# Six whole-array f-tiles instead of four in the opening of a squared-ReLU MLP

## The chip, the cores and the metric

The kernel runs on one core of a Trainium2 chip. The metric is the device time of one execution in microseconds (us). The profile is one execution, with a span about 1.7 us shorter than that execution's time. PE is the matrix engine, PEld its weight loads, DVE the vector engine, ACT the scalar engine, SP the engine that issues most of the transfers.

## The reference, cut

```python
# x (1, 2048, 576), w1 (576, 4608), b1 (4608), w2 (4608, 576), b2 (576), all bf16
h = jnp.einsum("bsd,df->bsf", x, w1) + b1
r = jnp.where(h > 0, h, 0)
h = r * r
out = jnp.einsum("bsf,fd->bsd", h, w2) + b2
```

The first product contracts 576 = 4 x 128 + 64 rows. The hidden width 4608 is 36 "f-tiles" of 128. The 2048 rows of x are worked in four blocks of 512.

## The kernel before

In most of the first product an f-tile is contracted in nine slices of 64 rows, and two f-tiles run side by side in the two halves of the array ("row-tiled"):

```python
def a_part(b, j, bk, steps):                  # a pair of f-tiles, 18 matmuls of 64x512
    for i in steps:
        for h in range(2):
            c = ORDER[h][i]
            rows = slice(h * H, (h + 1) * H)
            nc.tensor.matmul(bk[h][:], lhsT=w1h[rows, c, j * P:(j + 1) * P], rhs=xT[b][rows, place(h, c), :],
                             start=(i == 0), stop=(i == NH - 1))
```

This needs x transposed and copied to both halves of the partitions, so the kernel cannot begin with it. Block 0 begins with G = 4 f-tiles in another form, here called the opening: x arrives in four row tiles (x0 to x3), PE transposes them chunk by chunk, and each transposed chunk of 128 rows meets whole-array weights (chunks 0 to 3, each 128 rows by G f-tiles). It works in two halves of 256 columns, so that it can begin when only x0 and x1 are there:

```python
load_x(nc.sync, 0);    load_x(nc.scalar, 1)      # x tiles and weight chunks alternate on two queues
load_quad(nc.sync, 0); load_quad(nc.scalar, 1)
load_quad(nc.sync, 2); load_x(nc.scalar, 2)
load_x(nc.sync, 3);    load_quad(nc.scalar, 3)
...                                              # cut: remainder rows, then the row-tiled weights by pairs
bk0 = [bank("ph") for _ in range(G)]             # G of the 8 PSUM banks

def full_mm(half, c):
    cols = slice(half * HALF, (half + 1) * HALF)
    for q in range(4):
        nc.tensor.matmul(bk0[q][:, cols], lhsT=qn[:, c, q * P:(q + 1) * P], rhs=xT[0][:, c, cols], ...)

transpose_chunks(0, (0,), (V,));  transpose_chunks(0, (1,), (A,))    # each needs a PSUM bank and a copy out
transpose_chunks(0, (2,), (A,));  transpose_chunks(0, (NC,), (V,))
full_mm(0, 0)
transpose_chunks(0, (3,), (A,))
full_mm(0, 1); full_mm(0, 2)
transpose_chunks(1, (0, 1), (V, A))              # needs x2 and x3
full_mm(0, 3)
transpose_chunks(1, (2, NC), (A, V))
full_mm(1, 0)
transpose_chunks(1, (3,), (V,))
full_mm(1, 1)
...                                              # cut: biases
full_mm(1, 2); full_mm(1, 3)
...                                              # cut: remainder rows (64), two f-tiles side by side
```

Five dummy products ("warm", NWARM = 5) keep PE busy from 0.4 to 2.7 us, while x0 is on its way. Results leave PSUM through ACT (ReLU with bias) and DVE (square). After all four blocks the second product follows.

Of the kernel before, what the change touches and what calls it, by code (L numbers as in the profile page):

```python
# [17 lines left out]
def kernel(  # L18
# [9 lines left out]
    nc = tc.nc  # L28
    P = 128
    H = 64  # L30
    x2 = x.flatten_outer_dims()
    out2 = out.flatten_outer_dims()
    S, D = x2.shape
    F = w1.shape[1]
    FH = F // 2
    G = 4
    NFT = F // P
    NJ = NFT // 2
    NC = D // P
    NH = D // H  # L40
    DM = NC * P
# [15 lines left out]
    def bank(name):  # L57
        return psum.tile([P, SB], FP32, name=name, tag="bank")
# [10 lines left out]
    def early(n):  # L69
        at[0] += n  # L70
        assert at[0] <= NFT * D
        return w2_sb[:, at[0] - n:at[0]]


    xT = [early(XW).rearrange("p (w s) -> p w s", s=SB) for b in range(NSB - 1)]
    xT3 = xpool.tile([P, NH, SB], BF16, name="xT3", tag="xT3")
    xT.append(xT3[:])
    xs = early(RT * D).rearrange("p (j c) -> p j c", c=D)
    qn = early(NC * 4 * P).rearrange("p (c f) -> p c f", c=NC)
    qr = early(2 * P)  # L80
    pairs = [(0, 2), (1, 3)] + [(f, f + G) for f in range(G, NFT) if (f // G) % 2]
    slot = {ft: (h, j) for j, pr in enumerate(pairs) for h, ft in enumerate(pr)}
    assert len(pairs) == NJ and len(slot) == NFT

# [9 lines left out]
    def load_quad(eng, c):  # L94
        eng.dma_start(out=qn[:, c, :], in_=w1[c * P:(c + 1) * P, 0:G * P])

    def load_w1(eng, h, j0, n, cs):
        f0 = pairs[j0][h] * P
        eng.dma_start(out=w1h[h * H:(h + 1) * H, cs, j0 * P:(j0 + n) * P], in_=w1_rows[:, cs, f0:f0 + n * P])
# [1 line left out]
    NWARM = 5  # L101

    def load_rest(eng, h):
        eng.dma_start(out=qr[h * H:(h + 1) * H, :], in_=w1[DM:D, 2 * h * P:2 * (h + 1) * P])

    b1T = const.tile([P, NFT], FP32, name="b1T")
    warm = const.tile([P, 1], FP32, name="warm")
# [9 lines left out]
    for h in range(2):  # L117
        load_rest(nc.sync, h)


    for j0, n in ((2, 1), (3, 1), (4, 1), (5, 1), (6, 1), (7, 1), (8, 2), (10, 2), (12, 2), (14, 4)):
        for h in range(2):
            load_w1(nc.sync, h, j0, n, slice(0, NH))

# [46 lines left out]
    def copy_psum(eng, dst, src):  # L171
        if eng is nc.scalar:
            nc.scalar.copy(out=dst, in_=src)
        else:
            nc.vector.tensor_copy(out=dst, in_=src)  # L175

    def transpose_chunks(half, cs, engs):
        tps = [psum.tile([P, HALF], BF16, name="tp", tag="bank") for c in cs]
        for i in range(2):
            for c, tp in zip(cs, tps):  # L180
                d0 = c * P if c < NC else D - P
                nc.tensor.transpose(tp[:, i * P:(i + 1) * P], xs[:, 2 * half + i, d0:d0 + P], ident[:])  # L182
        cols = slice(half * HALF, (half + 1) * HALF)
        for c, tp, eng in zip(cs, tps, engs):
            copy_psum(eng, xT[0][:, c if c < NC else 7, cols], tp[:])
            if c == NC:
                nc.vector.tensor_copy(out=xT[0][0:H, 8, cols], in_=tp[H:P, :])

    def hT_of(b, ft):
        if b < NSB - 1:  # L190
            return hT[b][:, ft, :].rearrange("p (j s) -> p j s", j=RT)
        h, j = slot[ft]
        return w1h[:, h * RT:(h + 1) * RT, j * P:(j + 1) * P]

    def evac_h(b, ft, bk):
        r = rpool.tile([P, SB], BF16, name="r", tag="r")
        nc.scalar.activation(out=r[:], in_=bk[:], func=ACT.Relu, bias=b1T[:, ft:ft + 1], scale=1.0)  # L197
        r3 = r[:].rearrange("p (j s) -> p j s", j=RT)
        nc.vector.tensor_tensor(out=hT_of(b, ft), in0=r3, in1=r3, op=ALU.mult)  # L199

    def place(hi, c):
        if hi:
            return c // 2 if c % 2 else (3 + c // 2 if c else 8)
        return 8 if c == 8 else (4 if c % 2 else 0) + c // 2
# [11 lines left out]
    def a_step(b, j):  # L216
        bk = [bank("ph") for _ in range(2)]
        a_part(b, j, bk, range(NH))
        for h in range(2):
            evac_h(b, pairs[j][h], bk[h])  # L220


    bk0 = [bank("ph") for _ in range(G)]

    def full_mm(half, c):
        cols = slice(half * HALF, (half + 1) * HALF)
        for q in range(4):
            nc.tensor.matmul(bk0[q][:, cols], lhsT=qn[:, c, q * P:(q + 1) * P], rhs=xT[0][:, c, cols],  # L228
                             start=(half == 0 and c == 0), stop=False, skip_group_check=True)

    V, A = nc.vector, nc.scalar
    transpose_chunks(0, (0,), (V,))
    transpose_chunks(0, (1,), (A,))
    transpose_chunks(0, (2,), (A,))
    transpose_chunks(0, (NC,), (V,))
    full_mm(0, 0)
    transpose_chunks(0, (3,), (A,))
    full_mm(0, 1)
    full_mm(0, 2)
    transpose_chunks(1, (0, 1), (V, A))  # L240
    full_mm(0, 3)
# [6 lines left out]
    nc.vector.tensor_copy(out=b1T[:], in_=b1T_ps[:, 0:NFT])  # L248
    full_mm(1, 2)
    full_mm(1, 3)  # L250
    for i in range(2):
        for h in range(2):
            rows = slice(h * H, (h + 1) * H)
            nc.tensor.matmul(bk0[2 * h + i][:], lhsT=qr[rows, i * P:(i + 1) * P], rhs=xT[0][rows, place(h, 8), :],  # L254
                             start=False, stop=True, skip_group_check=True)
    nc.vector.tensor_copy(out=xT[0][0:H, 4:7, :], in_=xT[0][H:P, 0:3, :])
    nc.vector.tensor_copy(out=xT[0][H:P, 4:7, :], in_=xT[0][0:H, 1:4, :])
    nc.vector.tensor_copy(out=xT[0][H:P, 8, :], in_=xT[0][0:H, 0, :])
    for q in range(G):
        evac_h(0, q, bk0[q])  # L260


    def load_xT(b):
# [3 lines left out]

    load_xT(1)
    for h in range(2):
        load_w1(nc.sync, h, 0, 2, slice(0, NH))  # L270
    for b in range(2, NSB):
        load_xT(b)
    w2_view = w2_dram.rearrange("(ft p) d -> p ft d", p=P)
# [2 lines left out]
    def load_w2(c, n=1):  # L276
        nc.sync.dma_start(out=w2_sb[:, c * W2CH * D:(c + n) * W2CH * D].rearrange("p (ft d) -> p ft d", d=D),
                          in_=w2_view[:, c * W2CH:(c + n) * W2CH, :])
# [9 lines left out]
    def finish_xT(b):  # L288
        nc.vector.tensor_copy(out=xT[b][0:H, 8, :], in_=xT[b][H:P, 7, :])
        nc.vector.tensor_copy(out=xT[b][H:P, 8, :], in_=xT[b][0:H, 0, :])  # L290

    for j in range(2, NJ):
        a_step(0, j)
        if j == NJ - 2:
            finish_xT(1)
    load_w2(0)
    for b in range(1, NSB):
        for j in (*range(2, NJ), 0, 1):
            a_step(b, j)
            if j == NJ // 2 and b + 1 < NSB:  # L300
                finish_xT(b + 1)
        if b == 1:
            load_w2(1)
        if b == 2:
            load_w2(2, 2)
# [63 lines left out]
```

## Time and profile before

| | before |
|---|---|
| median time, three runs | 290.14 us |
| span of the profile | 288.7 us |
| PE busy | 284.9 us (99%) |
| opening, from the second x tile to the first row-tiled product | 3.09 to 9.78 us of the chain |
| 1260 row-tiled products | 135.97 us |

The page of the kernel before, its first lines; the number after x counts instructions:

```profile
span 288.7 us, 4818 instructions
...
PE 284.9 (99%) x2067; PEld 133.7 (46%) x2078; DVE 79.5 (28%) x196; ACT 95.6 (33%) x153; POOL 1.5 (1%) x8
...
PE   9999999999999999999999999999999999999996
```

PE is busy in every slice, and no other engine comes near. A share does not say what PE waits for, so the next view matters more: the chain of waits of the kernel before (start, length, what; the share of "by line" left out):

```profile
0.21 2.84 DMA w_sb<-in_x_dram
3.04 0.05 issue
3.09 0.93 PE tp L182 x7
4.02 0.85 PE ph L228 x4
4.87 0.21 PE tp L182 x2
5.09 1.36 PE ph L228 x8
6.45 0.22 PE tp L182 x4
6.67 0.44 PE ph L228 x4
...
9.24 0.54 PE ph L254 x4
9.78 135.97 PE ph L213 x1260
145.75 15.66 PE pc L315 x144
```

L182 are transposes, L228 the 256-column products, L254 the remainder rows, L213 the row-tiled products. One wait for x1 ends at 3.04 us; after that each piece follows the last. Four products take 0.85 us early and 0.44 us late: PE's clock is halved at first. The trace's record of the granted clock begins with full clock at 5.95 us. (The page's clock row shows full speed from the start: it knows only that record. In the opening, read the clock from the spacing of equal instructions: 213 ns slow, 109 ns fast.)

### The profile page before, as it was taken

To read this page: it belongs to the slowest core of one execution; us is meant where nothing else is said; L and a number is where in the kernel's file an instruction comes from. 1 tells how busy PE (TensorE), PEld (TensorE's weight loads), DVE (VectorE), ACT (ScalarE), POOL (GpSimd) and SP (SyncE) were. 2 spreads that over 40 slices of the span, in tenths; PEclk is the share of its full clock that TensorE was granted. 3 is DMA by queue.
4 is the path that set the end of the run, shared out by engine and by line. 5 is a ranking of instruction groups with operands and counts; after the bars stand their busy time and mean duration, and the time that the engine had idled before them with its cause. 6 is when DMAs were issued, how large, how long until landed. Compare 5 with 4: busy or idle time off the path is not lost.

```text
span 288.7 us, 4818 instructions
## 1 busy us (share of the span) xinstructions
PE 284.9 (99%) x2067; PEld 133.7 (46%) x2078; DVE 79.5 (28%) x196; ACT 95.6 (33%) x153; POOL 1.5 (1%) x8
## 2 busy tenths in 40 slices
PE   9999999999999999999999999999999999999996
PEld 5544444444444444444445444444444444444454
DVE  1644454444445444444420011111100111111111
ACT  3666666766666676666620000000000000000000
POOL 2000000000000000000000000000000000000000
PEclk9999999999999999999999999999999999999999
DMA  7999999910400004300000100000000000000000
GB/s 200 205 190 204 172 185 208 321 50 2 122 3 0 3 2 142 106 0 2 0 2 19 20 20 20 20 23 5 15 20 23 20 20 20 23 20 22 20 23 20
DMA packets 35381, 18.01 MB, mean 62 GB/s; under 512 B 21652, under 2 KB 35360, under 8 KB 35360
## 3 DMA queue, kind: packets, MB, share of 16 engines
q1 hardware_dynamic: 34752, 17.14, 26.4%
q10 hardware_dynamic: 576, 0.56, 0.6%
q8 instruction: 16, 0.26, 0.4%
q14 instruction: 5, 0.04, 0.0%
q0 software_dynamic: 32, 0.01, 0.0%
HBM read 11.94 MB, written 2.36 MB: 50 GB/s over the span
## 4 chain that ended last, share of the span: by engine, by line
PE 98%; DMA 1%; issue 0%; DVE 0%; ACTq 0%
PE ph L213 47%; PE po L329 43%; PE pc L315 5%; PE ph L228 2%; DMA w_sb<-in_x_dram 1%; PE tp L182 1%; PE ph L254 0%; DVE o_sb L331 0%; PE b1T_ps L247 0%; ACTq L353 0%
## 5 line engine op out<-in xcount | busy, mean ns | idle before, releaser
L197 ACT ACTIVATE r<-ph,b1T 128x512 bf16<-128x512 f32 x144 | 91.0, 685 | 48.4 <-PE ph L213 46.4
L213 PE MATMUL ph<-w_sb,w1h 64*128 64x512 bf16 x936 | 101.2, 376 | 0.0
L213 PEld LDWEIGHTS <-w1h 64*128 64x128 bf16 x1260 | 61.3, 94 | 74.6
L329 PE MATMUL po<-w_sb,hT 128*128 128x512 bf16 x423 | 92.9, 379 | 0.5
L329 PEld LDWEIGHTS <-hT 128*128 128x128 bf16 x432 | 42.2, 98 | 51.2 <-issue 0.4
L199 DVE TENSOR_TENSOR hT<-r 128x512 bf16<-128x512 bf16 x108 | 46.0, 426 | 54.7 <-ACT r L197 54.2
L331 DVE TENSOR_TENSOR o_sb<-po,b_bc 128x512 bf16<-128x512 f32 (+2 forms) x17 | 11.2, 660 | 116.7 <-PE po L329 109.7
L213 PE MATMUL ph<-xT,w1h 64*128 64x512 bf16 x324 | 35.1, 376 | 0.0
L329 PE MATMUL po<-w_sb,w1h 128*128 128x512 bf16 (+2 forms) x178 | 31.2, 336 | 0.1
L329 PEld LDWEIGHTS <-w1h 128*128 128x128 bf16 x180 | 16.2, 98 | 15.3
L199 DVE TENSOR_TENSOR w1h<-r 128x512 bf16<-128x512 bf16 x36 | 15.3, 426 | 19.6 <-ACT r L197 19.5
L315 PE MATMUL pc<-hT,w_sb 128*64 128x512 bf16 x108 | 15.7, 379 | 0.0
L315 PEld LDWEIGHTS <-w_sb 128*64 128x64 bf16 x144 | 8.1, 110 | 7.6 <-issue 0.4
L315 PE MATMUL pc<-w1h,w_sb 128*64 128x512 bf16 x36 | 7.9, 379 | 0.0
L317 ACT ACTIVATE oc<-pc,b2T 128x512 bf16<-128x512 f32 x2 | 1.4, 687 | 13.7 <-PE pc L315 13.7
L325 DVE COPY o_sb<-oc 128x64 bf16<-128x64 bf16 x16 | 2.8, 172 | 9.3 <-DMA oc<-oc 9.3
L228 PE MATMUL ph<-w_sb 128*128 128x256 bf16 x32 | 5.3, 313 | 0.0
L228 PEld LDWEIGHTS <-w_sb 128*128 128x128 bf16 x32 | 3.4, 115 | 0.6
L175 DVE COPY w_sb<-tp 128x256 bf16<-128x256 bf16 x5 | 1.5, 292 | 5.9 <-PE tp L182 5.9
L182 PE MATMUL tp<-ident,w_sb 128*128 128x128 bf16 x20 | 2.7, 264 | 0.1
L169 PE MATMUL wps<-one 128*128 128x512 bf16 x5 | 2.3, 628 | 0.4 <-DVE one L144 0.4
L182 PEld LDWEIGHTS <-w_sb 128*128 128x128 bf16 x20 | 1.9, 118 | 1.4 <-DMA w_sb<-in_x_dram 1.2
(27 smaller groups left out, 10.7 us busy)
## 6 DMA issues: line engine op xcount, KB each, us to landing
w_sb<-in_w_dram SPq DMA_DIRECT2D x2, 1728.0 KB, 8.7
w1h<-in_w_dram SPq DMA_DIRECT2D x8, 288.0 KB, 5.9
out_dram<-o_sb SPq DMA_DIRECT2D x15, 144.0 KB, 1.8
w1h<-in_w_dram SPq DMA_DIRECT2D x12, 144.0 KB, 3.7
w_sb<-in_w_dram SPq DMA_DIRECT2D x2, 864.0 KB, 7.2
w1h<-in_w_dram SPq DMA_DIRECT2D x2, 576.0 KB, 11.2
w_sb<-in_x_dram SPq DMA_DIRECT2D x2, 144.0 KB, 3.4
w_sb<-in_x_dram ACTq DMA_DIRECT2D x2, 144.0 KB, 3.5
```

Source lines behind the costliest of these rows:

```text
L169: nc.tensor.matmul(wps[:], lhsT=ones[:, 0:P], rhs=ones[:], start=(i == 0), stop=(i == NWARM - 1))
L175: nc.vector.tensor_copy(out=dst, in_=src)
L182: nc.tensor.transpose(tp[:, i * P:(i + 1) * P], xs[:, 2 * half + i, d0:d0 + P], ident[:])
L197: nc.scalar.activation(out=r[:], in_=bk[:], func=ACT.Relu, bias=b1T[:, ft:ft + 1], scale=1.0)
L199: nc.vector.tensor_tensor(out=hT_of(b, ft), in0=r3, in1=r3, op=ALU.mult)
L213: nc.tensor.matmul(bk[h][:], lhsT=w1h[rows, c, j * P:(j + 1) * P], rhs=xT[b][rows, place(h, c), :], start=(i == 0), stop=(i == NH - 1))
L228: nc.tensor.matmul(bk0[q][:, cols], lhsT=qn[:, c, q * P:(q + 1) * P], rhs=xT[0][:, c, cols], start=(half == 0 and c == 0), stop=False, ski ...
L315: nc.tensor.matmul(pc[h * H:(h + 1) * H, :], lhsT=w2(ft, DM, D), rhs=hT_of(2 * pr + h, ft), start=(ft == 0), stop=(ft == NFT - 1))
L317: nc.scalar.activation(out=oc[:, pr, :], in_=pc[:], func=ACT.Identity, bias=b2T[:], scale=1.0)
L325: nc.vector.tensor_copy(out=o_sb[:, DM:D], in_=o_tr[pr][:, jj, h * H:(h + 1) * H])
L329: nc.tensor.matmul(po[:, 0:e - a], lhsT=hT_of(b, ft)[:, jj, :], rhs=w2(ft, a, e), start=(ft == 0), stop=(ft == NFT - 1))
L331: nc.vector.tensor_tensor(out=o_sb[:, a:e], in0=po[:, 0:e - a], in1=b2_bc[:, a:e], op=ALU.add)
```

## The change

Its intent: let six f-tiles start in the form that is ready first, so that there is more work between transposes and so that the row-tiled weights are needed later; the bytes ahead of them on the queue stay the same. The diff, cut to its core (tables of pairs, remainder loads and loop bounds follow G in the same way, and the six results leave PSUM in the order in which they are finished):

```diff
-    G = 4
+    G = 6
+    GP = G // 2
...
-    qn = early(NC * 4 * P).rearrange("p (c f) -> p c f", c=NC)
+    qn = early(NC * G * P).rearrange("p (c f) -> p c f", c=NC)
...
-    for j0, n in ((2, 1), (3, 1), (4, 1), (5, 1), (6, 1), (7, 1), (8, 2), (10, 2), (12, 2), (14, 4)):
+    for j0, n in ((3, 1), (4, 1), (5, 1), (6, 1), (7, 1), (8, 1), (9, 1), (10, 2), (12, 2), (14, 4)):
...
-    bk0 = [bank("ph") for _ in range(G)]
...
-        for q in range(4):
+        for q in range(G):
...
-    transpose_chunks(0, (1,), (A,))
+    transpose_chunks(0, (1,), (V,))
     transpose_chunks(0, (2,), (A,))
     transpose_chunks(0, (NC,), (V,))
+    bk0 = [bank("ph") for _ in range(G)]
...
-        load_w1(nc.sync, h, 0, 2, slice(0, NH))
+        load_w1(nc.sync, h, 0, GP, slice(0, NH))
...
-    for j in range(2, NJ):
+    for j in range(GP, NJ):
```

Six accumulators leave two PSUM banks for the transposes. They are allocated after the first four transposes, whose banks two of them take over.

More of the change, by code (lines that the diff above doesn't have):

```diff
@@ L78 @@
     xs = early(RT * D).rearrange("p (j c) -> p j c", c=D)
-    qn = early(NC * 4 * P).rearrange("p (c f) -> p c f", c=NC)
-    qr = early(2 * P)
-    pairs = [(0, 2), (1, 3)] + [(f, f + G) for f in range(G, NFT) if (f // G) % 2]
+    qn = early(NC * G * P).rearrange("p (c f) -> p c f", c=NC)
+    qr = early(GP * P)
+    pairs = [(i, GP + i) for i in range(GP)] + [(G + i, G + NJ - GP + i) for i in range(NJ - GP)]
     slot = {ft: (h, j) for j, pr in enumerate(pairs) for h, ft in enumerate(pr)}
@@ L103, in load_rest @@
     def load_rest(eng, h):
-        eng.dma_start(out=qr[h * H:(h + 1) * H, :], in_=w1[DM:D, 2 * h * P:2 * (h + 1) * P])
+        eng.dma_start(out=qr[h * H:(h + 1) * H, :], in_=w1[DM:D, GP * h * P:GP * (h + 1) * P])
     b1T = const.tile([P, NFT], FP32, name="b1T")
@@ L250 @@
     full_mm(1, 3)
-    for i in range(2):
+    for i in range(GP):
         for h in range(2):
             rows = slice(h * H, (h + 1) * H)
-            nc.tensor.matmul(bk0[2 * h + i][:], lhsT=qr[rows, i * P:(i + 1) * P], rhs=xT[0][rows, place(h, 8), :],
+            nc.tensor.matmul(bk0[GP * h + i][:], lhsT=qr[rows, i * P:(i + 1) * P], rhs=xT[0][rows, place(h, 8), :],
                              start=False, stop=True, skip_group_check=True)
@@ L258 @@
     nc.vector.tensor_copy(out=xT[0][H:P, 8, :], in_=xT[0][0:H, 0, :])
-    for q in range(G):
-        evac_h(0, q, bk0[q])
+    for i in range(GP):
+        for h in range(2):
+            evac_h(0, GP * h + i, bk0[GP * h + i])
     def load_xT(b):
@@ L297 @@
     for b in range(1, NSB):
-        for j in (*range(2, NJ), 0, 1):
+        for j in (*range(GP, NJ), *range(GP)):
             a_step(b, j)
```

## The prediction

> **What bounds the kernel now.** The matrix engine, without a hole. The chain of waits has one wait, the load of the second x tile (0.21 to 3.04 us); from 3.09 to 285.97 us it is all PE, but for "issue" bits of 0.05 us. The page has PE 99% busy. The opening (transposes, whole-array products of 256-column halves, remainder rows) takes 3.09 to 9.78 us in the chain; then 1260 row-tiled matmuls take 135.97 us, 107.9 ns each.
>
> **What the change moves.** One pair of f-tiles leaves the row-tiled steps of block 0 and joins the opening.
> - Removed: 18 row-tiled matmuls, 18 x 107.9 ns = 1.94 us.
> - Added: 16 whole-array matmuls of 256 columns (the chain has 0.44 us for 4, so 109 ns) and 2 remainder ones: 1.96 us.
> Net +0.02 us. Both forms fill the array, and the opening has no idle time that more products could fill, so I see no gain.
>
> **The clock.** The clock record grants full clock only from 5.95 us: four 256-column matmuls take 0.85 us before it, 0.44 us after. The Trainium skill ("TensorE: Matmul & The Clock Gate", Part 1) says that the window is free-running; I expect the step at about the same time, and a stall before it to cost half its length.
>
> **Transfers.** Each whole-array weight chunk grows from 128 to 192 KB. By the issues' landings, x0, x1, chunk 0 and chunk 1 landed at 2.66, 3.05, 3.45 and 3.76 us, chunk 2 at 4.88, x2 5.27, x3 5.73, chunk 3 5.90. From 3.76 to 5.90 us 544 KB landed: 253 KB per us. The skill ("DMA: Bandwidth & Descriptors", Queues, rings and completion order) says that each DMA engine takes turns between queues, so chunk 0 pays for part of chunk 1. Estimates at that rate: chunk 0 at 3.8 us, chunk 1 4.3, chunk 2 5.6, x3 6.7, chunk 3 6.9. First uses, from the durations: chunk 0 at 3.71 us (slack before: 0.26 us), chunk 1 about 5.1, chunk 2 6.3, x3 6.9, chunk 3 7.1. Only the first is late, by 0.1 to 0.3 us in the slow clock; net 0.05 to 0.15 us. x1 may land 0.05 us later too.
>
> The bytes ahead of row-tiled pair 3 are unchanged, with two issues of 0.68 us fewer on the queue, so pair 3 (needed near 11.6 us as before) gains slack. The third deferred pair is needed only near 74 us.
>
> **PSUM.** Six accumulators leave two banks for transposes. From the last transpose's start to the end of ACT's copy was 0.63 us. Six matmuls between transposes take 0.66 us instead of 0.44, so the bank comes back just in time; perhaps 0.05 us is lost. Six evacuations queue 6 x 0.57 us on ACT, but the second row-tiled step needs only two, 1.94 us later: no stall.
>
> **Prediction.** 290.14 + 0.02 + 0.1 + 0.05 = about 290.3 us. The runs before spread over 0.9 us, so range 289.8 to 291.0. Faster by 2%: 0.01; within 2%: 0.97; slower: 0.02.
>
> **What would show it.** In the chain, 1242 row-tiled products from about 11.8 us, ending within 0.3 us of before; PE waiting 0.1 to 0.3 us for a DMA before its first whole-array product; no wait of PE on DVE or ACT over 0.1 us; the rest identical.
>
> **What would make it wrong.** Chunks landing in another order, so that several whole-array steps starve and the clock steps up later (up to 1.5 us); two transpose banks turning copies into waits at every step (up to 1 us); or the full clock coming at another time by its phase alone.

## The result, and the profile after

Ratios and intervals here are those of fast runs of the same rounds. They are not the ratios of the medians quoted, nor always those of the plain means of the runs listed, which give 1.0010 in run 1 and 1.0036 in run 4.

The changed kernel took 290.80 us in the median (290.07 to 290.97, 4 runs) against 290.11 us (4 runs): ratio 1.0015, 95% interval 0.9991 to 1.0039. Later rounds gave 290.07 us (5 runs, ratio 0.9995) and 290.23 us (6 runs, ratio 0.9993). The mean of all 15 runs of the changed kernel is 290.31 us; that of the 38 runs of the kernel before that were timed beside other kernels, in four sets of rounds, is 290.36 us.

The page of the changed kernel:

```profile
span 289.0 us, 4818 instructions
...
PE 285.2 (99%) x2067; PEld 134.6 (47%) x2078; DVE 79.6 (28%) x197; ACT 95.0 (33%) x152; POOL 1.5 (1%) x8
```

The chain of waits of the changed kernel (some lines are numbered one or two higher than before: the transposes are L183, the remainder rows L255, the row-tiled products L214):

```profile
0.21 2.74 DMA w_sb<-in_x_dram
...
2.99 0.93 PE tp L183 x7
3.92 1.28 PE ph L228 x6
...
5.41 1.93 PE ph L228 x12
7.35 0.22 PE tp L183 x4
7.57 0.66 PE ph L228 x6
...
11.23 0.75 PE ph L255 x6
11.99 134.03 PE ph L214 x1242
146.02 15.66 PE pc L317 x144
```

What the reader is to see: the same shape, each run of products 1.5 times as long, no wait of PE on DVE or ACT or on a weight chunk. The row-tiled products take 134.03 instead of 135.97 us, so 1.94 us less, and begin 2.21 us later. From the first row-tiled to the last product, by the starts in the trace, it is 276.095 us before and 274.153 after: 1.942 us less, which is 18 x 107.9 ns. Nothing else moved after the opening. So all of the 0.27 us by which this profile is longer (last product at 285.98 instead of 285.71 us) arises before 12 us.

It is not the added work. The first row-tiled product starts at: work at full clock + waits + half the sum of PE's start and the moment of the clock step, because PE does half as much until then. I take PE's start at the third transpose. Before: start 3.173, step 5.948, first row-tiled product 9.616 us, so 9.616 - (3.173 + 5.948)/2 = 5.056 us of work and waits. After: 3.073, 6.554 and 11.825 us, so 7.011 us. The difference is 1.955 us; the prediction had 1.96. Against the 1.942 us removed that is 0.013 us. The other 0.25 us are a clock step 0.61 us later, worth 0.30 us, less a start 0.10 us earlier, worth 0.05 us.

### The profile page after: what moved, and what is told of

It reads as the page before. It is cut to its first block, busy times and chain, and to the rows that moved or that the text cites. A ratio compares the mean times of both kernels' runs of the same rounds, so it can differ in the third digit from the quotient of the medians.

```text
span 289.0 us, 4818 instructions
## 1 busy us (share of the span) xinstructions
PE 285.2 (99%) x2067; PEld 134.6 (47%) x2078; DVE 79.6 (28%) x197; ACT 95.0 (33%) x152; POOL 1.5 (1%) x8
## 4 chain that ended last, share of the span: by engine, by line
PE 98%; DMA 1%; issue 0%; DVE 0%; ACTq 0%
PE ph L214 46%; PE po L331 43%; PE pc L317 5%; PE ph L228 2%; DMA w_sb<-in_x_dram 1%; PE tp L183 1%; PE ph L255 0%; DVE o_sb L333 0%; PE b1T_ps L248 0%; ACTq L355 0%
## 5 line engine op out<-in xcount | busy, mean ns | idle before, releaser
L214 PE MATMUL ph<-w_sb,w1h 64*128 64x512 bf16 x918 | 99.2, 376 | 0.0
L214 PEld LDWEIGHTS <-w1h 64*128 64x128 bf16 x1242 | 60.4, 94 | 73.6
L214 PE MATMUL ph<-xT,w1h 64*128 64x512 bf16 x324 | 35.1, 376 | 0.0
L228 PE MATMUL ph<-w_sb 128*128 128x256 bf16 x48 | 7.4, 310 | 0.0
L183 PE MATMUL tp<-ident,w_sb 128*128 128x128 bf16 x20 | 2.7, 264 | 0.1
L174 ACT COPY w_sb<-tp 128x256 bf16<-128x256 bf16 x4 | 1.5, 372 | 3.7 <-PE tp L183 3.6
```

The lines of the kernel that those rows point to most:

```text
L174: nc.scalar.copy(out=dst, in_=src)
L183: nc.tensor.transpose(tp[:, i * P:(i + 1) * P], xs[:, 2 * half + i, d0:d0 + P], ident[:])
```

## The experiments

Two theories stood at this point. One: the change itself costs nothing, and executions differ because the clock step falls at a random phase. The rival: the change costs about 0.4 us of its own, in wider chunks or scarcer banks, which the profile happens not to show. In runs 1, 2, 10, 11 and 12 the kernel is unchanged but for one or two comment lines on top, which raise line numbers. Runs 1 to 4, 5 to 8 and 9 to 12 were made on three different chips, each set beside runs of the kernel before on the same chip. So a ratio compares kernels on one chip, but profiles of different sets come from different chips (that of the first two profiles is not on record).

### 1. The kernel before, again (e1_before_again)

```diff
+# control: the kernel before, again
```

> The kernel before, unchanged: a null comparison. Theory (the step to full clock falls at a random phase; the change itself costs 0.02 us): its time spreads by about 0.9 us from execution to execution, ratio 1.000 with an interval of about 0.002 to each side; in the profile the span equals 288.7 us plus half the shift of the clock step from 5.95 us, plus the shift of the first two-tile transposes from 3.09 us, within 0.05 us. Rival (the change costs about 0.4 us of its own): no spread beyond 0.3 us within one kernel.

Measured: 290.55 us median, 290.00 to 292.37 us, 6 runs; ratio to the other runs of the same kernel 1.0015, interval 0.9993 to 1.0036. A null comparison thus gave the very ratio that the change had given. The rival is not needed for a 0.15% difference, and one kernel alone spreads by more than 2 us, where 0.9 was expected.

The second half of the expectation failed. This trace has no clock record; by the spacing, full clock came at 4.45 us, 1.5 us earlier than in the first profile, with a start 0.3 us earlier. By the expectation the span should have fallen to 287.6 us. That counts the earlier start in full; with half of it, as in the sum above, it would be 287.8. It was 288.5 us. The timeline of PE shows where the rest went (start, length, what, the idle time before it in brackets):

```profile
4.45 0.60 PE L229 MATMUL ph<-w_sb 128*128 128x256 bf16 x4
5.39 0.61 PE L229 MATMUL ph<-w_sb 128*128 128x256 bf16 x4 [0.34 <-DMA w_sb<-in_w_dram]
```

With the fast clock PE caught up with the transfers and stood still until chunk 2 landed, at 5.34 us. By the distance of starts it lost 0.50 us there and 0.16 us more for x3. So the phase theory lacked a term: an early step is partly given back in waits.

### 2. The changed kernel, again (e2_after_again)

```diff
+# control: the changed kernel, again
```

> The changed kernel, unchanged, beside the null. Theory: ratio within 0.9990 to 1.0010 over enough executions, and the profiled span equals 289.0 us plus half the shift of the clock step from 6.55 us and the shift of the PE start from 2.99 us. Rival (the change itself costs 0.4 us or more): ratio 1.0015 again with an interval clear of 1, and a longer span even with an early clock step.

Measured: 290.07 us median, 289.81 to 290.60, 5 runs; ratio 0.9995, interval 0.9982 to 1.0008. The rival's 0.4 us (0.14%) is outside the interval.

Here full clock was granted already at 3.45 us, 3.11 us earlier than in the first profile of this kernel. By the sum above the span should have been 289.0 - 3.11/2 - 0.33/2 = 287.2 us (the expectation counts the start in full: 287.1); it was 288.8. The timeline of PE, and then the waits of PE for weights from 2 to 12 us (waiter, releaser, us in total, times, longest; weight loads and products are listed apart, so their totals overlap):

```profile
3.88 0.83 PE L229 MATMUL ph<-w_sb 128*128 128x256 bf16 x6 [0.30 <-DMA w_sb<-in_w_dram]
...
4.87 0.83 PE L229 MATMUL ph<-w_sb 128*128 128x256 bf16 x6
6.16 0.83 PE L229 MATMUL ph<-w_sb 128*128 128x256 bf16 x6 [0.47 <-DMA w_sb<-in_w_dram]
```

```profile
PEld L229 <- DMA w_sb<-in_w_dram: 1.5, 3, 0.7
PE ph L229 <- DMA w_sb<-in_w_dram: 0.8, 2, 0.5
```

PE waited for chunk 0 (landed 3.84 us), chunk 1 (4.82), chunk 2 (6.11) and chunk 3 (7.16). The idle time in brackets understates it, as the ends of matmuls are modelled; by the distance of starts the losses are 0.50, 0.20, 0.63 and 0.11 us, and 0.04 for x3, 1.48 in all. The sum above gives 11.635 - (2.743 + 3.445)/2 = 8.541 us, 1.53 us over the 7.011 of work. The two agree within 0.05 us, and they account for the gap in the span. Of the 1.55 us that the earlier step was worth, the waits took back 1.5.

### 3. Two f-tiles in the opening (e3_two_tiles)

```diff
-    G = 6
+    G = 2
-    for j0, n in ((3, 1), (4, 1), ...
+    for j0, n in ((1, 1), (2, 1), (3, 1), (4, 1), ...
```

> Only two whole-array f-tiles (the change's code with G = 2, pair 1 loaded first). Theory: the opening is worth what waits it avoids. With two products (0.22 us) between transposes the copies from PSUM, 0.29 to 0.37 us plus hand-over, are no longer hidden, and row-tiled pair 1 is needed near 7.7 us while its two loads landed at 7.4 and 8.4 us before in that place: PE waits 0.5 to 1.0 us in all, the time rises by 0.3 to 0.9 us. If there is no wait, the time is as before within 0.1 us.

Measured: 291.64 us median, 291.39 to 291.90, 5 runs; ratio 1.0047, interval 1.0035 to 1.0059. So the opening does earn time, and the direction was right; at about 1.2 us (mean 291.66 against 290.44 us; 1.0 to 1.7 by the interval) the size is above the expected 0.9. The waits of PE in this trace that are not for x tiles, from 2 to 40 us (columns as above):

```profile
PEld L214 <- DMA w1h<-in_w_dram: 0.9, 2, 0.4
PEld L228 <- DMA w_sb<-in_w_dram: 0.4, 1, 0.4
...
PE ph L228 <- DVE w_sb L176: 0.2, 1, 0.2
```

All three suspected kinds are there: a copy from PSUM not hidden, a chunk, and row-tiled weights that land late, both the first pair (8.44 us) and the last group of four pairs (33.81 us). From the first row-tiled to the last product it is 278.474 us; 276.095 + 1.942 = 278.037 would be the work, so 0.44 us are lost there, 0.31 on the first pair and 0.12 on the last group by the distance of starts. The opening holds 3.430 us where 5.056 - 1.955 = 3.101 were work: 0.33 us more. That is 0.77 us of the 1.2; the rest I did not settle (this profile's step, at 6.58 us, was late, and no other execution was profiled).

### 4. Wider chunks, the surplus unused (e4_wide_chunks)

```diff
-    qn = early(NC * G * P)...
+    qn = early(NC * 8 * P)...
-        eng.dma_start(out=qn[:, c, :], in_=w1[c * P:(c + 1) * P, 0:G * P])
+        eng.dma_start(out=qn[:, c, :], in_=w1[c * P:(c + 1) * P, 0:8 * P])
```

> The changed kernel with each of its four chunks read 8 f-tiles wide (256 instead of 192 KB), the surplus unused: doubles the change's extra bytes and nothing else. Theory (the transfers have a few tenths of slack left): chunk 3 landed at 6.91 us against a need of 7.41; with 256 KB more it lands near 7.9 us, so PE waits about 0.3 to 0.6 us for a DMA in the opening and the time rises by that. Rival (early transfers are far from limiting): no wait, time as after within 0.1 us.

Measured: 291.53 us median, 290.47 to 292.42, 6 runs; ratio 1.0045, interval 1.0024 to 1.0065. The rival of this expectation falls: the same products with 64 KB more per chunk cost over 1 us. The profiled execution was one of the quicker ones, with the clock step at 6.40 us. It waited for chunk 0 (0.26 us of slow clock, so half of that) and for chunk 3 (0.14 us; landed 7.43 us), and the opening holds 7.277 us, 0.27 more than the work. That explains an execution of 290.8 us, but not the mean. That the slower ones had earlier steps and longer waits, as in run 2, is argued, not shown.

### 5 and 6. Two banks for the transposes, and a control (e5_two_transpose_banks, e6_order_8_banks)

Run 6 is the kernel before with the change's order of allocation and its second copy on DVE; run 5 is run 6 with a PSUM pool of 6 banks.

```diff
-    psum = ctx.enter_context(tc.tile_pool(name="psum", bufs=8, space=PSUM))
+    psum = ctx.enter_context(tc.tile_pool(name="psum", bufs=6, space=PSUM))      # run 5 alone
-    bk0 = [bank("ph") for _ in range(G)]
-    transpose_chunks(0, (1,), (A,))
+    transpose_chunks(0, (1,), (V,))
     transpose_chunks(0, (2,), (A,))
     transpose_chunks(0, (NC,), (V,))
+    bk0 = [bank("ph") for _ in range(G)]
```

> Four whole-array f-tiles as before, but a PSUM pool of 6 banks, so two are left for the transposes as in the changed kernel, with 4 products (0.44 us) between transposes instead of 6 (0.66 us). Theory (the transpose of two tiles frees its bank 0.63 us after its last matmul started, so 0.66 us is just enough and 0.44 us is not): PE waits about 0.2 us before the transposes after the third half-step, and again one step later; time up 0.2 to 0.5 us. Rival (banks are not close to limiting): no wait of PE on DVE or ACT, time as before.

> Control for the run with 6 banks: the same order of allocation and the second copy on DVE, but 8 banks. Both theories: no wait, time as the kernel before, ratio 0.999 to 1.001 but for the clock step's phase.

Measured: run 5 290.32 us (5 runs, ratio 1.0002, interval 0.9989 to 1.0015); run 6 290.39 us (6 runs, ratio 0.9994, interval 0.9981 to 1.0006). In time neither differs from the kernel before, and so two pieces of the change, the order of allocation and the engine of the second copy, show no effect of their own, within 0.2%. In the trace of run 5 a transpose twice waited for ACT's copy of an earlier tile: it started 0.14 us late at 3.97 us and 0.13 us late at 7.00 us (the copy ended at 6.95). Below is the second place, in the timelines of run 5 and then of run 6; from the four products to the transposes it is 0.57 and 0.44 us:

```profile
6.43 0.60 PE L227 MATMUL ph<-w_sb 128*128 128x256 bf16 x4
7.00 0.27 PE L182 MATMUL tp<-ident,w_sb 128*128 128x128 bf16 x2
```

```profile
6.26 0.60 PE L227 MATMUL ph<-w_sb 128*128 128x256 bf16 x4
6.70 0.28 PE L182 MATMUL tp<-ident,w_sb 128*128 128x128 bf16 x2
```

Run 6 and all three profiles of the changed kernel have no such wait. So 0.44 us of products between transposes are not enough for two banks and 0.66 us are, as predicted, but the waits were smaller than the expected 0.2 us, came after the first and the fifth run of products instead of the third and the fourth, and were too small to be measured in the time.

These two profiles also add early steps. In run 6 it came at 3.93 us; PE lost 0.17 us waiting for x3 and the span was 287.8 us, the shortest of all profiles. In run 5 it came at 3.32 us, and the opening holds 5.947 us, 0.89 over the work, of which 0.80 are seen as waits for x2, x3, chunk 3 and the copies.

### 7 and 8. No dummy products, and six (e7_no_warm_products, e8_six_warm_products)

```diff
-    NWARM = 5
+    NWARM = 0        # run 7; run 8 has 6
```

Run 7 also leaves out the PSUM tile that the dummy products wrote.

> The kernel before without the five dummy products that keep PE busy from 0.4 to 2.7 us. Theory[...]: PE is first busy at about 2.7 us, so the step comes about 2 us later, near 6.5 to 9 us, and the time rises by half of that, about 1 us. Rival (the clock steps at a phase that does not depend on activity so soon): no change.

> The kernel before with six dummy products instead of five, so that PE is busy without the gap of 0.3 us before the second x tile landed. If that gap delays the clock step, it comes earlier (by up to some tenths, or a window) and the time falls by half of that; if not, the time rises by at most 0.1 us, as the sixth product ends near 3.1 us.

Measured: run 7 290.65 us (5 runs, ratio 1.0012, interval 1.0000 to 1.0024), run 8 290.33 us (6 runs, ratio 0.9997, interval 0.9982 to 1.0012). PE's first instruction of run 7 is at 2.34 us, and the step came at 6.73 us. By the means the five dummy products are worth about 0.35 us (0 to 0.7 by the interval), not 1 us. Closing the gap of 0.3 us earns nothing that can be measured. The Trainium skill ("TensorE: Matmul & The Clock Gate", Part 1) says that full clock is granted after a busy window of about 3.4 us that is free-running; all recorded steps here lie 2.9 to 6.2 us after PE's first instruction (steps at 3.32 to 6.58 us with PE busy from 0.38 us; 4.4 us after it in run 7), a spread of 3.3 us, which fits a random phase within one such window. That the whole window must be busy does not fit: in runs 5, 2 and 10 the step came 2.9, 3.1 and 3.2 us after PE's first instruction. The window itself stands in the traces: in the 13 that have a clock record, of whatever kernel, full clock lasted 283.306 us (10 times) or 286.720 us (3 times), which differ by 3.414 us and are 83 and 84 times 3.4133 us, to 3 ns. So its end falls on the same grid as its start, and one kernel meets this grid at different phases: the changed one at 3.45, 3.56 and 6.55 us.

### 9. The change's products with the old chunk bytes (e9_narrow_chunks)

```diff
-        eng.dma_start(out=qn[:, c, :], in_=w1[c * P:(c + 1) * P, 0:G * P])
+        eng.dma_start(out=qn[:, c, 0:4 * P], in_=w1[c * P:(c + 1) * P, 0:4 * P])
-            nc.tensor.matmul(bk0[q][:, cols], lhsT=qn[:, c, q * P:(q + 1) * P], ...
+            nc.tensor.matmul(bk0[q][:, cols], lhsT=qn[:, c, q % 4 * P:(q % 4 + 1) * P], ...
```

> The changed kernel's products, but chunks of only 4 f-tiles are loaded, as before the change; the products of tiles 4 and 5 read tiles 0 and 1 again, so the result is wrong on purpose. Undoes the extra bytes of the chunks alone. Theory (with an early clock step the opening runs into the transfers, and wider chunks make that worse; with a step after 6 us there is no wait): in the profile the opening, counted at full clock (half the slow time plus the fast time from the third transpose to the first row-tiled product), is 7.01 us plus at most 0.3 us of waits for x tiles or chunks, whatever the step; the mean time is below the changed kernel's by 0.1 to 0.4 us. Rival (the bytes do not matter): the same time as the changed kernel within 0.1 us and waits of the same size.

Measured, with a wrong result as intended: 289.77 us median, 289.58 to 290.88, 6 runs; ratio to the kernel before 0.9989, interval 0.9973 to 1.0006. Its mean is 0.13 us below that of the changed kernel in the same rounds (290.06 against 290.19 us), inside the noise: in time this is inconclusive. In the profile the step came at 4.45 us, chunk 3 landed at 6.19 us, and PE waited for nothing; the opening holds 7.037 us. The changed kernel has no profile with a step near 4.45 us to set beside it, so the pair shows that bytes move the landings, not by how much they move the mean.

### 10, 11, 12. More looks at both kernels (e10_after_look, e11_before_look, e12_before_look2)

```diff
+# changed look 1      (run 10; runs 11 and 12: the kernel before with such a line)
```

> The changed kernel once more, for the landings and the clock step of another execution, and more times. Theory: the opening counted at full clock is 7.01 us plus the waits for transfers seen in it, within 0.06 us; the waits are zero when the step comes after about 6 us and 1 us or more when it comes before 4 us. Ratio 0.999 to 1.002.

> The kernel before once more, one look. Theory: the opening counted at full clock is 5.06 us plus the waits for transfers seen in it, within 0.06 us; with a clock step before 4.5 us there are 0.2 to 0.7 us of waits, with one after 5.5 us at most 0.1. From the first row-tiled to the last product 276.10 us as in every profile of it.

> As the look before it: 5.06 us plus the seen waits within 0.06 us; 276.10 us from the first row-tiled to the last product.

Measured: the changed kernel 290.23 us (6 runs, ratio 0.9993, interval 0.9980 to 1.0006); the looks at the kernel before 290.25 and 290.24 us, one run each. Run 10 had its step at 3.56 us. The chain of waits there no longer begins with x, but with chunk 3:

```profile
1.59 5.33 DMA w_sb<-in_w_dram
6.92 0.05 issue
6.96 0.83 PE ph L229 x6
7.79 0.22 PE tp L184 x4
```

Waits for chunk 2, x3 and chunk 3 cost 0.14, 0.17 and 0.72 us by the distance of starts, 1.03 in all; the sum gives 1.12 us, a miss of the 0.06 us that I had allowed. Part of that is the formula's: a slow product takes 213 ns, not twice 109. Runs 11 and 12 had their steps at 5.73 and 5.59 us, no wait above 0.1 us, 5.08 and 5.10 us in the opening and 276.096 us from the first row-tiled to the last product.

All profiles of the two kernels together, in us; "over work" is what the opening holds beyond 5.056 us before and 7.011 us after:

| profile | clock step | chunk 3 landed | over work | waits seen | span |
|---|---|---|---|---|---|
| before, first | 5.95 | 5.90 | (reference) | none | 288.7 |
| before, run 1 | 4.45 (by spacing) | 6.23 | 0.68 | 0.66 | 288.5 |
| before, run 11 | 5.73 | 6.24 | 0.02 | none | 288.5 |
| before, run 12 | 5.59 | 6.23 | 0.04 | none | 288.5 |
| after, first | 6.55 | 6.91 | (reference) | none | 289.0 |
| after, run 2 | 3.45 | 7.16 | 1.53 | 1.48 | 288.8 |
| after, run 10 | 3.56 | 6.92 | 1.12 | 1.03 | 288.5 |

The steps differ by 3 us, worth 1.5 us of PE's time; the spans differ by 0.5 us. At an early step the changed kernel's opening lost more (1.53 and 1.12 us) than the old products did in runs 1, 6 and 5 (0.68, 0.27 and 0.89 us with steps at 4.45, 3.93 and 3.32; about 0.3 of run 5's are bank waits). As steps and chips differ, that the wider chunks cost some tenths in such executions is possible and not shown.

## Why the prediction was right

- "Net +0.02 us ... so I see no gain": right. The work grew by 1.955 - 1.942 = 0.013 us. The kernel was bound by PE's stream before and after, both forms fill the array, and moving work from one to the other moves nothing. The Trainium skill ("TensorEngine Tiling (Array Packing)", Key Properties) says that a change of tiling mode drains the engine. Both traces fit this: the step into the remainder rows takes 0.205 us between starts where 0.109 is usual. The change adds no such step.
- "The rest identical": right to 1 ns (274.153 against 276.095 - 1.942 us).
- "1242 row-tiled products from about 11.8 us, ending within 0.3 us of before": right, 11.83 us by the starts (11.99 in the chain that the prediction named), and 0.27 us.
- Chunk 0 late, "PE waiting 0.1 to 0.3 us for a DMA before its first whole-array product": wrong for the profile, where chunk 0 landed at 3.47 us instead of the estimated 3.8. It landed at 3.84 and 3.37 us in the two later profiles of the changed kernel. The estimate took one mean rate from one execution as if it were fixed, while even the unchanged kernel had chunk 0 at 3.13 to 3.45 us. The estimate for chunk 3 (6.9 us) held: 6.91, 7.16 and 6.92 us. In part this is luck: in the profile on record chunk 1, chunk 2 and x3 landed at 3.97, 5.08 and 6.17 us, 0.3 to 0.5 us before their estimates.
- "I expect the step at about the same time": this step of the argument failed, and it does not follow from the free-running window that the prediction cites, which can meet a kernel at any phase. The recorded steps range from 3.32 to 6.73 us. The prediction named it as a risk, and it is what moves single executions. It also made "only the first is late" wrong: with a step before 4 us, chunks 2 and 3 and the x tiles are late, up to 1.5 us in all. The total still held because the step gives PE what the waits then take.
- PSUM "just in time; perhaps 0.05 us is lost": right in substance; nothing was lost, and run 5 shows that two thirds of the products would have been too few.
- Slack of the row-tiled weights: right. Pair 3's second load landed at 8.56 instead of 9.93 us against a need of 11.8 (before 11.6). The last group landed at 30.35 instead of 32.69 us, needed at about 33.2 and 32.9 us by the first start and 1.942 us per pair. In these two profiles a slack of 0.2 us turned into 2.8; in the later ones, counted alike, it is 1.2 to 1.9 us before and 2.6 and 2.9 after. This slack is the change's real gift, but nobody was waiting. In run 3, where the first pair and that group were late, they cost 0.31 and 0.12 us.
- The number, "about 290.3 us": the 15 runs have a mean of 290.31 us, but the kernel before has 290.36. Of the 0.17 us that were added to 290.14, the profile shows only the 0.013; the 0.1 us for chunk 0 and the 0.05 us for PSUM did not occur in it. That the mean fits so closely is luck, and the range given (289.8 to 291.0 us) takes in every median of either kernel.

What stays open: what the change costs or gains in the mean below 0.2%, as the last two ratios' intervals reach from 0.9980 to 1.0008; what sets the phase of the clock step; and the single slow executions (292.37 and 291.69 us of the unchanged kernel), none of which was profiled.

## What to carry to other kernels

Count the engine's instructions between two fixed points before and after: when the bound engine has no hole, moving work between two equally dense forms cannot pay, however sensible the reasons. More overlap pays up to the point where the waits are gone (two f-tiles to four: about 1.2 us), and nothing beyond it (four to six: no difference within 0.2%). Take a few profiles of the same kernel before explaining tenths of a microsecond, and run the null comparison: here it gave the same 1.0015 as the change.

## What the Trainium skill lacked or had wrong

- "TensorE: Matmul & The Clock Gate", Part 1, gives the moment of the clock step as about 4 us into sustained activity, give or take 0.5 us. Here, with PE first busy at 0.38 us in each, it was recorded from 3.32 to 6.58 us, a range of 3.3 us, which is nearer to the whole window of 3.4 us that the same page describes; the least wait, 2.9 us after PE's first instruction, is shorter than that window.
- The same page, Part 4, says that full clock does not engage for PE transposes. Here the kernel's transposes start 107 ns apart before the step and 56 ns after it, nearly in the same ratio as products (213 and 109 ns). The trace lists them as matmuls without their mode, and no run tests whether they count as activity for the step.
- No page says that an early clock step can be worth nothing: in the changed kernel a step at 3.45 instead of 6.55 us was worth 1.55 us of PE's time, and 1.5 us of it were spent waiting for weights.
- "DMA: Bandwidth & Descriptors" gives costs per transfer but no spread. The landing of the same 128 KB chunk 0 of the same kernel, issued at 0.5 us, varied from 3.13 to 3.45 us over four executions, and that of chunk 3 from 5.90 to 6.24 us. These were not all on one chip; runs 11 and 12, which were, have 3.18 and 3.29, 6.24 and 6.23 us.
